# Placing the held and the streamed operand of the large products in different parts of SBUF

## The chip, the cores and the metric

One core of a Trainium2 chip runs the whole program. The metric is device time in microseconds (us), the median of a few executions. A profile of one execution gives the time of every instruction on the five engines: TensorE (PE, with its weight loads as PEld), VectorE (DVE), ScalarE (ACT), GpSimd (POOL) and SyncE (SP, which here issues the DMAs).

A product on TensorE has two operands in SBUF. One is loaded into the array first and stays there; this text calls it the held operand (`lhsT` in the code, the weight load of the profile). The other is then streamed through the array (`rhs`). While one product streams, the held operand of the next one is loaded.

## The reference, cut to what matters

```python
x = attn(q, k, v, p)               # 4 x 576 tokens, 8 heads of 64 -> (2304, 512)
h = x @ w_in;  x = (h * cos(h)) @ w_out               # 512 -> 2048 -> 512, float64 weights
P = exp(x @ w_gate - max); 8 times: rows and columns of P normalised   # 8 experts
out = sum_e P[:, e:e+1] * (relu(x @ w1[e]) @ w2[e])   # 512 -> 1024 -> 512 each
```

Products are made at higher than single-pass precision: each operand is kept as two float32r parts, high and low, and a product is three matmuls (high with high, high with low, low with high).

## The kernel before

The program has three parts. **Attention** (about the first 110 us) is interleaved by a hand-written table, `ORDER`, with the start of the second part. **The first feed-forward layer** runs over 4 slices of its hidden width (`u` below `U1`); each takes the 2304 tokens in 8 chunks of 288 columns (`HC`). `in_g1` (L506 to L508) makes the hidden values, `in_g2` (L565) the output, which is summed in `acc`. **The experts** (`u` from 4 to 19: 16 units, two halves of each of 8 experts) take the tokens in 3 chunks (`j`) of 768. `g1_mult` (L723) forms the first product of an expert as 7 block products per chunk (a Strassen-like scheme, `MULTS`), each of 12 matmuls with 384 columns streamed. `out_tile` (L793 to L795) forms the second product, 6 tiles per chunk of 12 matmuls with 512 columns streamed. In the expert loop of `tile_kernel` a tile of the chunk before stands behind each of the block products 2 to 7 of a chunk (none behind the first), so TensorE's order is: block product, block product, tile, block product, tile, and so on.

The operands of these products:

- in `g1_mult` the held operand is a piece of `w1` (`w_slot`), the streamed one a piece of the transformed tokens (`x_slot`, four of them, refilled by two DMAs each from `xd` in DRAM, `x_load`);
- in `out_tile` the held operand is a piece of the hidden values, out of one of six slots (`slots`: three tiles `slot0` to `slot2` and three pieces of `hreg`), which `relu_split` fills by one ACT and one DVE instruction; the streamed one is `w2` (`whi`, `wlo` of pool `wp`);
- in `in_g2` the held operand is `whi` or `wlo`, the streamed one `hreg`; in `in_g1` both are in `xh` and `xl`.

In the profile the streamed operand is named first: `bank<-whi,hreg` streams `whi` and holds `hreg`. `xh` and `xl` have four planes of 2304 columns. Planes 0 and 1 hold the attention weights of the tokens and later the four `x_slot`s (and, in their last 768 columns, `w_slot`s 9 to 11); planes 2 and 3 hold the mixed weights of the first layer and later `w_slot`s 0 to 8.

Pools are placed from the low end of a partition upward, or from the high end downward (`side="right"`). In the built program of before, the buffers lie at these bytes of each partition:

| buffer | bytes | role in the large products |
|---|---|---|
| `xh`, `xl` | 1,152 to 74,880 | both operands of L506 to L508 and of L723 |
| `hreg` | 77,696 to 100,736 | streamed in L565, held in L793 to L795 |
| `whi`, `wlo` (6 each) | 102,592 to 114,880, 114,880 to 127,168 | held in L565, streamed in L793 to L795 |
| `pp`, `rbuf`, `tail`, `mag`, `val`, later `slot0` to `slot2` | 139,456 to 158,656 | slots: held in L793 to L795 |
| sums, `acc`, first-layer `w1` pieces, raw `w1` (right side) | 161,760 to 229,344 | few products |

Of the kernel before, what the change touches and what calls it, by code (L numbers as in the profile page):

```python
# [8 lines left out]
F32 = mybir.dt.float32  # L9
F32R = mybir.dt.float32r  # L10
# [4 lines left out]
ALU = mybir.AluOpType  # L15
# [3 lines left out]
P = 128  # L19
B, H, S, HD = 4, 8, 576, 64  # L20
NP = 32
NT, DM = 2304, 512
KD = DM // P
# [4 lines left out]
HC = 288  # L28

HT = 384  # L30
NJ = 3
TQ = HT // P
# [72 lines left out]
def tile_kernel(ctx: ExitStack, tc: tile.TileContext, qT, kT, v, pT, w_in, w_out, w_gate, w1, w2, out):  # L105
    nc = tc.nc

    const = ctx.enter_context(tc.tile_pool(name="const", bufs=1))
    small = ctx.enter_context(tc.tile_pool(name="small", bufs=2))
    wp = ctx.enter_context(tc.tile_pool(name="wp", bufs=6))  # L110
    pools = {"w1h": ctx.enter_context(tc.tile_pool(name="w1hp", bufs=6, side="right"))}
# [2 lines left out]

    xh = const.tile([P, KD, NT], F32R, name="xh")
    xl = const.tile([P, KD, NT], F32R, name="xl")
    ident = const.tile([P, P], F32, name="ident")
    ones = const.tile([P, P], F32, name="ones")  # L120
    wg = const.tile([P, KD, E], F32, name="wg")
# [1 line left out]
    lg = const.tile([P, NT // P, E], F32, name="lg")  # L123
    prob = const.tile([P, NT // P, E], F32, name="prob")
    bank = psp.tile([P, 8, 512], F32, name="bank")
    hreg = const.tile([P, 5 * 4 * HC], F32R, name="hreg")
    first = ctx.enter_context(ExitStack())
    cvp = first.enter_context(tc.tile_pool(name="cvp", bufs=1))
    pp = cvp.tile([P, KD, B, 64], F32, name="pp")
# [97 lines left out]
    class Attention:  # L227
# [179 lines left out]
            return x[:, g, S * b:S * b + S]  # L407

        def f_hi(self, i):
            nc.scalar.copy(self.f_dst(xh, i), self.g[i]["a2T"])  # L410

        def f_lo(self, i):
            nc.vector.tensor_tensor(
                out=self.f_dst(xl, i), in0=self.g[i]["a2T"],
                in1=self.f_dst(xh, i).bitcast(F32), op=ALU.subtract,
            )


# [1 line left out]
    def mix_col(b):  # L420
        return S * b + 64 * (b % 2)
# [2 lines left out]


    def pp_hi(j):
        x = (xh, xl)[j // 2][:, 2 + j % 2, :]
        return x.rearrange("p (a s) -> p a s", s=2 * S)[:, :, 512:512 + P]

    def mix_split(j):  # L430
        full = pp[:, j].rearrange("p (a b) n -> p a (b n)", a=2)
        nc.scalar.copy(pp_hi(j), full)
        nc.vector.tensor_tensor(
            out=pools["ppl"][:, j], in0=full, in1=pp_hi(j).bitcast(F32), op=ALU.subtract
        )

    def mix_mm(ps, u, m):
        if u < 2:
            b, g = divmod(m, 2)
# [12 lines left out]
        nc.tensor.matmul(ps, lhsT=pl, rhs=wh, start=False, stop=True)  # L452

    def mix_parts(u, m):
        if u < 2:
            b, g = divmod(m, 2)
            return [(slice(0, P), 2 + g, slice(mix_col(b), mix_col(b) + 512))]
        bp, j = divmod(m, KD)
        parts = []
        for h in range(2):  # L460
            o = mix_col(2 * bp + (h ^ (j % 2)))
            parts.append((slice(64 * h, 64 * h + 64), 2 + j // 2, slice(o, o + 512)))
        return parts

    def mix_hi(ps, u, m):
        for rows, plane, cols in mix_parts(u, m):
            nc.scalar.copy(xh[rows, plane, cols], ps[rows, :])

    def mix_lo(ps, u, m):
        for rows, plane, cols in mix_parts(u, m):  # L470
            nc.vector.tensor_tensor(
                out=xl[rows, plane, cols], in0=ps[rows, :],
                in1=xh[rows, plane, cols].bitcast(F32), op=ALU.subtract,
            )

    def acc_cols(t0, n):

        i, o = divmod(t0, NA)
        return acc[i].rearrange("p (k n) -> p k n", n=NA)[:, :, o:o + n]

    h_sb = {}
# [4 lines left out]
    def ps_g1(s):  # L486
        return pair(g1_pair.get(s, s % 2))
# [5 lines left out]
    def unit_step(s):  # L493
        return s // 16, (s % 16) // 2, s % 2

    def in_g1(s):
        u, c, p = unit_step(s)
        ps = ps_g1(s)
        t0 = HC * c
        for fi in range(2):  # L500
            o = mix_col(c // 2) + P * (2 * p + fi)
            for g in range(2):
                mh, ml = xh[:, 2 + g, o:o + P], xl[:, 2 + g, o:o + P]
                ah, al = xh[:, g, t0:t0 + HC], xl[:, g, t0:t0 + HC]
                dst = ps[:, fi, 0:HC]
                nc.tensor.matmul(dst, lhsT=mh, rhs=ah, start=(g == 0), stop=False)  # L506
                nc.tensor.matmul(dst, lhsT=mh, rhs=al, start=False, stop=False)
                nc.tensor.matmul(dst, lhsT=ml, rhs=ah, start=False, stop=(g == 1))  # L508

    def in_hi(s):  # L510
        u, c, p = unit_step(s)
# [69 lines left out]

    def x_slot(n):
        cols = slice(HT * n, HT * n + HT)
        return xh[:, 0:2, cols], xl[:, 0:2, cols]

    def w_slot(q):
        r, o = (2, 256 * q) if q < 9 else (0, 4 * HT + 256 * (q - 9))
        return xh[:, r:r + 2, o:o + 256], xl[:, r:r + 2, o:o + 256]


    def way_slot(z):
        cols = slice(1024 + HT * z, 1024 + HT * z + HT)
        return xh[:, 2:4, cols], xl[:, 2:4, cols]

    xd = ctx.enter_context(tc.tile_pool(name="xdp", bufs=1, space=bass.MemoryType.DRAM)).tile(
        [7 * NJ, P, 2, 2 * HT], F32, name="xd"
# [5 lines left out]
    def halves(t):  # L602
        return t.rearrange("p (a n) -> p a n", a=2)
# [99 lines left out]
        put(2, a12)  # L703

    def next_h():
        slot = slots.pop(0)
        return slot, halves(slot[:, 0:2 * HT]), halves(slot[:, 2 * HT:4 * HT])

    def two_banks(b):
        return bank[:, 2 * b:2 * b + 2, 0:HT]  # L710
# [16 lines left out]
        x_load()  # L727

    def relu_split(src, th, q, hb):
        slot, hi, lo = next_h()  # L730
        nc.scalar.activation(hi, src, AF.Relu)  # L731
        nc.vector.scalar_tensor_tensor(
            out=lo, in0=src, scalar=0.0, in1=hi.bitcast(F32), op0=ALU.max, op1=ALU.subtract
        )
        hb[q, th] = (hi, lo, slot)

    def g1_steps(u, j):

# [34 lines left out]
    def out_g2(u, j, i):  # L773
        parts = 2 if u == NU - 1 and j == NJ - 1 and i == 2 * TQ - 1 else 1
        for part in range(parts):
            out_tile(u, j, i, part, KD // parts)
        if i % TQ == TQ - 1:
            slots.extend(h_sb[u, j][q, i // TQ][2] for q in range(2))

    def out_tile(u, j, i, part, width):  # L780

        t = 2 * TQ * j + i
        e, half = divmod(u - U1, 2)
        planes = slice(part * width, part * width + width)
        ps = bank[:, 4 + counts["bank"] % 3, 0:P * width]
        counts["bank"] += 1
        th, o = divmod(i, TQ)
        for f in range(4):
            wh, wl = (w[:, P * planes.start:P * planes.stop] for w in w_sb[u, 2, f])
            p, q = divmod(f, 2)  # L790
            hi, lo, _ = h_sb[u, j][q, th]
            a, bq = hi[:, p, P * o:P * o + P], lo[:, p, P * o:P * o + P]
            nc.tensor.matmul(ps, lhsT=a, rhs=wh, start=(f == 0), stop=False)  # L793
            nc.tensor.matmul(ps, lhsT=a, rhs=wl, start=False, stop=False)  # L794
            nc.tensor.matmul(ps, lhsT=bq, rhs=wh, start=False, stop=(f == 3))  # L795
        ps = ps.rearrange("p (k n) -> p k n", n=P)
        dst = acc_cols(P * t, P)[:, planes, :]
        if e == 0:
            if half == 0:
                nc.scalar.copy(dst, ps)  # L800
            else:
                nc.vector.tensor_tensor(out=dst, in0=ps, in1=dst, op=ALU.add)
            return
# [70 lines left out]
    side = []  # L874
# [9 lines left out]
    with tc.manual_schedule():  # L884
# [14 lines left out]
        def in_front(s):  # L899
            in_g1(s)  # L900
            in_turns(s)
            if s > 0:
                in_hi(s - 1)
                in_lo(s - 1)
            if s >= 4:
                in_acc(s - 4)
            in_rest(s)
            if s in convert:
                convert[s]()
# [147 lines left out]
        in_acc(n1 - 4)  # L1057
        first.close()
        op = ctx.enter_context(tc.tile_pool(name="op", bufs=1))
        slots = [op.tile([P, 4 * HT], F32R, name=f"slot{i}") for i in range(3)]  # L1060
        slots += [hreg[:, 4 * HT * i:4 * HT * i + 4 * HT] for i in range(3)]
        l_sb = op.tile([P, HT], F32, name="l_sb")


# [91 lines left out]
```

## Time and profile before

| | |
|---|---|
| median of 3 runs | 1926.49 us (1925.85 to 1928.16) |
| the profiled execution | 1925.82 us, of which its span from first to last instruction is 1924.0 us |
| TensorE busy | 1890.1 us of the span (98%), 11113 matmuls |
| DVE, ACT, POOL busy | 952.2, 595.6 and 505.1 us |
| chain that ended last | TensorE 77% of the span: L723 36%, L793 to L795 41% |
| mean granted TensorE clock | 0.995 of full |

The profile's page gives busy times and groups of instructions; the busy time of TensorE counts matmuls that overlap, and the end of each matmul is modelled, so the mean duration of a matmul is no measure of its pace. The pace is read from the timeline, as the distance between the starts of successive matmuls.

### The profile page before, as it was taken

How to read it: one execution, taken by the hardware profiler on the slowest of the kernel's cores; microseconds unless marked ns; L12 is line 12 of the kernel's file. 1: busy time of each engine (PE TensorE's matmuls, PEld its weight loads, DVE VectorE, ACT ScalarE, POOL GpSimd, SP SyncE). 2: the span in 40 equal slices, each digit the busy share in tenths (PEclk: the TensorE clock that was granted, in tenths of full speed). 3: DMA queues.
4: the chain of work that ended last, by engine and by line, in shares of the span. 5: the costliest groups of instructions: out<-in, count | busy, mean ns of one | idle time of the engine just before them, and what ended most of it. 6: DMA issues, size and time to landing. Idle time of an engine off the chain costs nothing.

```text
span 1924.0 us, 27227 instructions
## 1 busy us (share of the span) xinstructions
PE 1890.1 (98%) x11113; PEld 1711.4 (89%) x11113; DVE 952.2 (49%) x1239; ACT 595.6 (31%) x911; POOL 505.1 (26%) x382
## 2 busy tenths in 40 slices
PE   6999999988999999999999999999999999999999
PEld 4799999977998999989999999999899989999998
DVE  6867776564554563444434343434344443434343
ACT  5877777632321121212122121212121212121210
POOL 3445454520322222221212131303030303030300
PEclk9999999999999999999999999999999999999999
DMA  8511111189665656565666666666666666656564
GB/s 297 159 45 56 45 55 45 58 270 306 198 224 169 228 173 225 172 226 182 214 196 208 200 191 203 201 203 188 204 204 204 196 209 188 215 181 216 185 200 116
DMA packets 229772, 348.89 MB, mean 181 GB/s; under 512 B 14480, under 2 KB 209168, under 8 KB 229648
## 3 DMA queue, kind: packets, MB, share of 16 engines
q1 hardware_dynamic: 229648, 347.15, 56.4%
q8 instruction: 88, 1.44, 0.3%
q14 instruction: 36, 0.29, 0.0%
HBM read 325.86 MB, written 21.23 MB: 180 GB/s over the span
## 4 chain that ended last, share of the span: by engine, by line
PE 77%; DVE 2%; DMA 1%; ACT 1%; POOL 0%; issue 0%; SPq 0%; POOLq 0%; DVEq 0%; ACTq 0%
PE bank L723 36%; PE bank L794 14%; PE bank L793 14%; PE bank L795 13%; DMA xd<-xl 1%; DVE xl L620 1%; DMA xd<-xh 0%; DVE sum L613 0%; DVE rbuf L533 0%; ACT rbuf L538 0%; ACT rbuf L541 0%; DVE rbuf L546 0%; DVE acc L576 0%; PE bank L825 0%; PE bank L565 0%
## 5 line engine op out<-in xcount | busy, mean ns | idle before, releaser
L723 PE MATMUL bank<-xh 128*128 128x384 f32 x1344 | 456.1, 339 | 2.5 <-DVE rbuf L546 2.5
L723 PE MATMUL bank<-xl,xh 128*128 128x384 f32 x1344 | 453.4, 337 | 0.0
L723 PE MATMUL bank<-xh,xl 128*128 128x384 f32 x1344 | 453.0, 337 | 0.0
L747 DVE TENSOR_TENSOR sum<-bank,sum 128x768 f32<-128x768 f32 x240 | 229.8, 957 | 382.8 <-PE bank L723 382.7
L681 POOL TENSOR_TENSOR xl<-wraw,xh 128x512 fp32r<-128x512 f32 x112 | 158.1, 1412 | 701.8 <-ACT xh L680 646.2
L806 DVE SCALAR_TENSOR_TENSOR acc<-bank,prob,acc 128x512 f32<-128x512 f32 (+1 forms) x253 | 189.0, 747 | 189.9 <-PE bank L795 188.8
L723 PEld LDWEIGHTS bank<-xh 128*128 128x128 f32 x1344 | 253.2, 188 | 19.1 <-issue 3.7
L723 PEld LDWEIGHTS bank<-xl,xh 128*128 128x128 f32 x1344 | 253.7, 189 | 10.0
L723 PEld LDWEIGHTS bank<-xh,xl 128*128 128x128 f32 x1344 | 253.4, 189 | 0.0
L794 PE MATMUL bank<-wlo,hreg 128*128 128x512 f32 x580 | 228.1, 393 | 0.0
L795 PE MATMUL bank<-whi,hreg 128*128 128x512 f32 x580 | 226.1, 390 | 0.0
L793 PE MATMUL bank<-whi,hreg 128*128 128x512 f32 x580 | 225.8, 389 | 0.0
L793 PE MATMUL bank<-whi,slot 128*128 128x512 f32 x576 | 224.8, 390 | 0.0
L794 PE MATMUL bank<-wlo,slot 128*128 128x512 f32 x576 | 224.7, 390 | 0.0
L795 PE MATMUL bank<-whi,slot 128*128 128x512 f32 x576 | 224.1, 389 | 0.0
L223 POOL TENSOR_TENSOR wlo<-raw,whi 128x512 fp32r<-128x512 f32 x64 | 86.8, 1367 | 440.0 <-ACT whi L222 440.0
L565 PE MATMUL bank<-hreg,whi 128*128 128x288 f32 x1024 | 187.0, 294 | 0.2 <-DVE rbuf L546 0.2
L731 ACT ACTIVATE hreg<-sum 128x768 fp32r<-128x768 f32 x72 | 61.0, 847 | 374.3 <-DVE sum L747 374.3
L731 ACT ACTIVATE slot<-sum 128x768 fp32r<-128x768 f32 x72 | 60.9, 846 | 369.6 <-DVE sum L747 369.6
L565 PEld LDWEIGHTS bank<-hreg,whi 128*128 128x128 f32 x1024 | 153.1, 188 | 2.0 <-DVE rbuf L546 1.1
L795 PEld LDWEIGHTS bank<-whi,hreg 128*128 128x128 f32 x580 | 108.9, 188 | 23.7
L795 PEld LDWEIGHTS bank<-whi,slot 128*128 128x128 f32 x576 | 108.1, 188 | 23.2
(143 smaller groups left out, 2482.0 us busy)
## 6 DMA issues: line engine op xcount, KB each, us to landing
xh<-xd SPq DMA_DIRECT2D x332, 384.0 KB, 3.4
xl<-xd SPq DMA_DIRECT2D x332, 384.0 KB, 4.0
raw<-w SPq DMA_DIRECT2D x32, 512.0 KB, 6.0
wraw<-w SPq DMA_DIRECT2D x64, 256.0 KB, 5.1
raw<-w_in SPq DMA_DIRECT2D x16, 512.0 KB, 3.7
raw<-w_out SPq DMA_DIRECT2D x16, 512.0 KB, 3.7
xd<-xh SPq DMA_DIRECT2D x21, 384.0 KB, 5.1
xd<-xl SPq DMA_DIRECT2D x21, 384.0 KB, 5.5
```

Of the source, the lines that this page charges most:

```text
L223: nc.gpsimd.tensor_tensor(out=lo, in0=raw, in1=hi.bitcast(F32), op=ALU.subtract)
L565: nc.tensor.matmul(ps[:, di, 0:HC], lhsT=lhsT, rhs=rhs, start=(n in (0, 6)), stop=(n in (17, 23)),)
L620: nc.vector.tensor_tensor(out=lo, in0=src[m], in1=hi.bitcast(F32), op=ALU.subtract)
L681: nc.gpsimd.tensor_tensor(out=lo, in0=src, in1=hi.bitcast(F32), op=ALU.subtract)
L723: nc.tensor.matmul(dst, lhsT=w, rhs=t[:, k, :], start=start and k == 0 and w is a and t is th, stop=k == 1 and w is bq, skip_group_check=True,
L731: nc.scalar.activation(hi, src, AF.Relu)
L747: nc.vector.tensor_tensor(out=out, in0=ps, in1=other, op=ALU.add)
L793: nc.tensor.matmul(ps, lhsT=a, rhs=wh, start=(f == 0), stop=False)
L794: nc.tensor.matmul(ps, lhsT=a, rhs=wl, start=False, stop=False)
L795: nc.tensor.matmul(ps, lhsT=bq, rhs=wh, start=False, stop=(f == 3))
L806: nc.vector.scalar_tensor_tensor(out=dst, in0=ps, scalar=prob[:, t, e:e + 1], in1=dst, op0=ALU.mult, op1=ALU.add)
```

## The change

`xh` and `xl` are taken apart. Planes 0 and 1 become `ah` and `al`, planes 2 and 3 become `mh` and `ml`. `ah`, `al` and `hreg` go into a new pool `upper` at the high end of the partition; `mh` and `ml` stay at the low end. `hreg` grows from 5760 to 6144 columns, so that it has four slots for the experts in place of three. The other two slots for hidden values are now columns 1536 to 2304 of `ah` and `al`, where `w_slot`s 9 to 11 were; those move into a new tile `more`, low in the partition, on the bytes that `pp`, `rbuf` and part of `tail` leave free when the first layer ends. `slot0` to `slot2` are gone.

```diff
     const = ctx.enter_context(tc.tile_pool(name="const", bufs=1))
+    upper = ctx.enter_context(tc.tile_pool(name="upper", bufs=1, side="right"))
...
-    xh = const.tile([P, KD, NT], F32R, name="xh")
-    xl = const.tile([P, KD, NT], F32R, name="xl")
+    ah = upper.tile([P, 2, NT], F32R, name="ah")
+    al = upper.tile([P, 2, NT], F32R, name="al")
+    hreg = upper.tile([P, 16 * HT], F32R, name="hreg")
+    mh = const.tile([P, 2, NT], F32R, name="mh")
+    ml = const.tile([P, 2, NT], F32R, name="ml")
...
-    hreg = const.tile([P, 5 * 4 * HC], F32R, name="hreg")
...
     def x_slot(n):
         cols = slice(HT * n, HT * n + HT)
-        return xh[:, 0:2, cols], xl[:, 0:2, cols]
+        return ah[:, :, cols], al[:, :, cols]
 
     def w_slot(q):
-        r, o = (2, 256 * q) if q < 9 else (0, 4 * HT + 256 * (q - 9))
-        return xh[:, r:r + 2, o:o + 256], xl[:, r:r + 2, o:o + 256]
+        if q < 9:
+            cols = slice(256 * q, 256 * q + 256)
+            return mh[:, :, cols], ml[:, :, cols]
+        rest = more[:, q - 9]
+        return halves(rest[:, 0:512]), halves(rest[:, 512:1024])
...
-        slots = [op.tile([P, 4 * HT], F32R, name=f"slot{i}") for i in range(3)]
-        slots += [hreg[:, 4 * HT * i:4 * HT * i + 4 * HT] for i in range(3)]
+        more = op.tile([P, 3, 1024], F32R, name="more")
+        slots = [(ah[:, :, HT * i:HT * i + HT], al[:, :, HT * i:HT * i + HT]) for i in (4, 5)]
+        for i in (3, 0, 1, 2):
+            slot = hreg[:, 4 * HT * i:4 * HT * i + 4 * HT]
+            slots.append((halves(slot[:, 0:2 * HT]), halves(slot[:, 2 * HT:4 * HT])))
```

The rest of the diff renames: what read or wrote planes of `xh` and `xl` now names `ah`, `al`, `mh`, `ml`.

Every engine carries out the same instructions in the same order with the same shapes as before; no matmul, DMA or vector instruction is added, removed or moved. Apart from names, the built programs differ in a handful of waits at the start of the experts: the first write of `more` on ACT waits for GpSimd's last use of `rbuf` (L522 of before), where the first write of `slot0` did; two of DVE's writes into the new fourth piece of `hreg` and its first write of `l_sb` wait for GpSimd as well; GpSimd loses one wait for TensorE.

The bytes of each partition after the change:

| buffer | bytes | role in the large products |
|---|---|---|
| `mh`, `ml` | 1,152 to 38,016 | held in L506 to L508 and in L723 |
| `whi`, `wlo` | 42,688 to 54,976, 54,976 to 67,264 | held in L565, streamed in L793 to L795 |
| `pp`, `rbuf`, `tail`, `mag`, `val`, later `more` | 79,552 to 98,752 | `more`: held in L723 |
| sums, `acc`, first-layer `w1` pieces, raw `w1` | 100,320 to 167,904 | few products |
| `ah`, `al` | 167,904 to 204,768 | streamed in L506 to L508 and in L723; two slots held in L793 to L795 |
| `hreg` | 204,768 to 229,344 | streamed in L565; four slots held in L793 to L795 |

## Rows read from the trace of the kernel before

**Rows 1.** The page: span, busy us per engine (share, instructions), TensorE's granted clock.

```profile
span 1924.0 us, 27227 instructions
PE 1890.1 (98%) x11113; PEld 1711.4 (89%) x11113; DVE 952.2 (49%) x1239; ACT 595.6 (31%) x911; POOL 505.1 (26%) x382
...
PEclk9999999999999999999999999999999999999999
```

**Rows 2.** The page's chain that ended last: shares of the span by engine and line.

```profile
PE 77%; DVE 2%; DMA 1%; ACT 1%; POOL 0%; issue 0%; SPq 0%; POOLq 0%; DVEq 0%; ACTq 0%
PE bank L723 36%; PE bank L794 14%; PE bank L793 14%; PE bank L795 13%; DMA xd<-xl 1%; DVE xl L620 1%; DMA xd<-xh 0%; DVE sum L613 0%; DVE rbuf L533 0%; ACT rbuf L538 0%; ACT rbuf L541 0%; DVE rbuf L546 0%; DVE acc L576 0%; PE bank L825 0%; PE bank L565 0%
```

**Rows 3.** TensorE's waits: who waited for whom, us in total, times, longest.

```profile
PE bank L825 <- DVE lg L816: 7.5, 5, 5.6
PE bank L267 <- DMA k<-kT: 6.6, 3, 4.4
...
PE bank L723 <- DVE rbuf L546: 2.5, 1, 2.5
```

**Rows 4.** The page's costliest groups: out<-in, shapes, count | busy us, mean ns.

```profile
L723 PE MATMUL bank<-xh 128*128 128x384 f32 x1344 | 456.1, 339 | 2.5 <-DVE rbuf L546 2.5
...
L793 PE MATMUL bank<-whi,hreg 128*128 128x512 f32 x580 | 225.8, 389 | 0.0
L793 PE MATMUL bank<-whi,slot 128*128 128x512 f32 x576 | 224.8, 390 | 0.0
...
L565 PE MATMUL bank<-hreg,whi 128*128 128x288 f32 x1024 | 187.0, 294 | 0.2 <-DVE rbuf L546 0.2
L731 ACT ACTIVATE hreg<-sum 128x768 fp32r<-128x768 f32 x72 | 61.0, 847 | 374.3 <-DVE sum L747 374.3
L731 ACT ACTIVATE slot<-sum 128x768 fp32r<-128x768 f32 x72 | 60.9, 846 | 369.6 <-DVE sum L747 369.6
```

**Rows 5.** Timeline of TensorE in the experts (start us, modelled us): beginnings of groups of 12.

```profile
997.11 0.39 PE L793 MATMUL bank<-whi,slot 128*128 128x512 f32 x1
...
999.84 0.34 PE L723 MATMUL bank<-xh 128*128 128x384 f32 x1
...
1001.95 0.33 PE L723 MATMUL bank<-xh 128*128 128x384 f32 x1
...
1004.03 0.39 PE L793 MATMUL bank<-whi,hreg 128*128 128x512 f32 x1
...
1006.78 0.34 PE L723 MATMUL bank<-xh 128*128 128x384 f32 x1
...
1018.61 0.39 PE L793 MATMUL bank<-whi,slot 128*128 128x512 f32 x1
...
1021.33 0.34 PE L723 MATMUL bank<-xh 128*128 128x384 f32 x1
```

**Rows 6.** The same timeline: a tile that begins in `hreg` and alternates with a slot.

```profile
706.67 0.39 PE L793 MATMUL bank<-whi,hreg 128*128 128x512 f32 x1
...
707.37 0.40 PE L793 MATMUL bank<-whi,slot 128*128 128x512 f32 x1
...
708.07 0.39 PE L793 MATMUL bank<-whi,hreg 128*128 128x512 f32 x1
...
708.76 0.39 PE L793 MATMUL bank<-whi,slot 128*128 128x512 f32 x1
...
709.44 0.34 PE L723 MATMUL bank<-xh 128*128 128x384 f32 x1
```

**Rows 7.** The same timeline: 24 matmuls of L565, from their first to the next L723.

```profile
400.90 0.43 PE L565 MATMUL bank<-hreg,whi 128*128 128x288 f32 x2
...
404.06 0.34 PE L723 MATMUL bank<-xh 128*128 128x384 f32 x1
```

**Rows 8.** Timelines of POOL, ACT and DVE where the experts start.

```profile
390.53 1.43 POOL L522 TENSOR_TENSOR hreg<-rbuf,hreg 128x576 fp32r<-128x576 f32 x1 [3.03 <-ACT hreg L516]
...
405.41 0.62 ACT L680 CAST xh<-wraw 128x512 fp32r<-128x512 f32 x1
...
415.86 0.96 DVE L732 SCALAR_TENSOR_TENSOR slot<-sum,slot 128x768 fp32r<-128x768 f32 x1 [1.79 <-ACT slot L731]
```

More of the change, by code (lines that the diff above doesn't have):

```diff
@@ L409, in f_hi @@
         def f_hi(self, i):
-            nc.scalar.copy(self.f_dst(xh, i), self.g[i]["a2T"])
+            nc.scalar.copy(self.f_dst(ah, i), self.g[i]["a2T"])
         def f_lo(self, i):
             nc.vector.tensor_tensor(
-                out=self.f_dst(xl, i), in0=self.g[i]["a2T"],
-                in1=self.f_dst(xh, i).bitcast(F32), op=ALU.subtract,
+                out=self.f_dst(al, i), in0=self.g[i]["a2T"],
+                in1=self.f_dst(ah, i).bitcast(F32), op=ALU.subtract,
             )
@@ L426, in pp_hi @@
     def pp_hi(j):
-        x = (xh, xl)[j // 2][:, 2 + j % 2, :]
+        x = (mh, ml)[j // 2][:, j % 2, :]
         return x.rearrange("p (a s) -> p a s", s=2 * S)[:, :, 512:512 + P]
@@ L456, in mix_parts @@
             b, g = divmod(m, 2)
-            return [(slice(0, P), 2 + g, slice(mix_col(b), mix_col(b) + 512))]
+            return [(slice(0, P), g, slice(mix_col(b), mix_col(b) + 512))]
         bp, j = divmod(m, KD)
@@ L461, in mix_parts @@
             o = mix_col(2 * bp + (h ^ (j % 2)))
-            parts.append((slice(64 * h, 64 * h + 64), 2 + j // 2, slice(o, o + 512)))
+            parts.append((slice(64 * h, 64 * h + 64), j // 2, slice(o, o + 512)))
         return parts
@@ L466, in mix_hi @@
         for rows, plane, cols in mix_parts(u, m):
-            nc.scalar.copy(xh[rows, plane, cols], ps[rows, :])
+            nc.scalar.copy(mh[rows, plane, cols], ps[rows, :])
     def mix_lo(ps, u, m):
@@ L471, in mix_lo @@
             nc.vector.tensor_tensor(
-                out=xl[rows, plane, cols], in0=ps[rows, :],
-                in1=xh[rows, plane, cols].bitcast(F32), op=ALU.subtract,
+                out=ml[rows, plane, cols], in0=ps[rows, :],
+                in1=mh[rows, plane, cols].bitcast(F32), op=ALU.subtract,
             )
@@ L502, in in_g1 @@
             for g in range(2):
-                mh, ml = xh[:, 2 + g, o:o + P], xl[:, 2 + g, o:o + P]
-                ah, al = xh[:, g, t0:t0 + HC], xl[:, g, t0:t0 + HC]
+                wh, wl = mh[:, g, o:o + P], ml[:, g, o:o + P]
+                th, tl = ah[:, g, t0:t0 + HC], al[:, g, t0:t0 + HC]
                 dst = ps[:, fi, 0:HC]
-                nc.tensor.matmul(dst, lhsT=mh, rhs=ah, start=(g == 0), stop=False)
-                nc.tensor.matmul(dst, lhsT=mh, rhs=al, start=False, stop=False)
-                nc.tensor.matmul(dst, lhsT=ml, rhs=ah, start=False, stop=(g == 1))
+                nc.tensor.matmul(dst, lhsT=wh, rhs=th, start=(g == 0), stop=False)
+                nc.tensor.matmul(dst, lhsT=wh, rhs=tl, start=False, stop=False)
+                nc.tensor.matmul(dst, lhsT=wl, rhs=th, start=False, stop=(g == 1))
     def in_hi(s):
@@ L583, in x_slot @@
         cols = slice(HT * n, HT * n + HT)
-        return xh[:, 0:2, cols], xl[:, 0:2, cols]
+        return ah[:, :, cols], al[:, :, cols]
     def w_slot(q):
-        r, o = (2, 256 * q) if q < 9 else (0, 4 * HT + 256 * (q - 9))
-        return xh[:, r:r + 2, o:o + 256], xl[:, r:r + 2, o:o + 256]
+        if q < 9:
[3 more added lines that the diff above has]
+        return halves(rest[:, 0:512]), halves(rest[:, 512:1024])
     def way_slot(z):
         cols = slice(1024 + HT * z, 1024 + HT * z + HT)
-        return xh[:, 2:4, cols], xl[:, 2:4, cols]
+        return mh[:, :, cols], ml[:, :, cols]
     xd = ctx.enter_context(tc.tile_pool(name="xdp", bufs=1, space=bass.MemoryType.DRAM)).tile(
@@ L705, in next_h @@
     def next_h():
-        slot = slots.pop(0)
-        return slot, halves(slot[:, 0:2 * HT]), halves(slot[:, 2 * HT:4 * HT])
+        return slots.pop(0)
     def two_banks(b):
@@ L729, in relu_split @@
     def relu_split(src, th, q, hb):
-        slot, hi, lo = next_h()
+        hi, lo = next_h()
         nc.scalar.activation(hi, src, AF.Relu)
@@ L734, in relu_split @@
         )
-        hb[q, th] = (hi, lo, slot)
+        hb[q, th] = (hi, lo)
     def g1_steps(u, j):
@@ L777, in out_g2 @@
         if i % TQ == TQ - 1:
-            slots.extend(h_sb[u, j][q, i // TQ][2] for q in range(2))
+            slots.extend(h_sb[u, j][q, i // TQ] for q in range(2))
     def out_tile(u, j, i, part, width):
@@ L790, in out_tile @@
             p, q = divmod(f, 2)
-            hi, lo, _ = h_sb[u, j][q, th]
+            hi, lo = h_sb[u, j][q, th]
             a, bq = hi[:, p, P * o:P * o + P], lo[:, p, P * o:P * o + P]
```

## The prediction, made before the changed kernel ran

> **What bounds the kernel now.** The page comes first: TensorE is busy for 98% of the span and its granted clock stands at full in every slice [rows 1], which is the upper of its two levels, 2.4 GHz. The chain that ended last lies on TensorE for 77% of the span, 36% in L723 and 41% in L793 to L795 [rows 2]. TensorE's waits come next: the three largest are 7.5, 6.6 and 2.5 us, all at the start of the program or of the experts [rows 3]. So in the experts, some 1500 us, nothing but the pace of the matmuls sets the time, and a change that only moves buffers can act in one way alone: it changes that pace.
>
> The grouped view doesn't show the pace. It gives 389 and 390 ns for a 512-column matmul that holds `hreg` or a slot [rows 4], but these ends are modelled and the matmuls overlap. The starts in the timeline do show it. A block product (12 matmuls of 384 columns) that follows another block product takes 1004.03 - 1001.95 = 2.08 us, or 173.3 ns a matmul. One that follows a tile takes 1001.95 - 999.84 = 2.11 [rows 5]. Tiles (12 matmuls of 512 columns) come in four kinds, by the places of their held operands: all in slots 1021.33 - 1018.61 = 2.72 us, which is 226.7 ns a matmul; slot first, then `hreg`, 999.84 - 997.11 = 2.73; all in `hreg` 1006.78 - 1004.03 = 2.75 [rows 5]; `hreg` first, then slot, 709.44 - 706.67 = 2.77 [rows 6]. The instructions are the same; the addresses differ, and so does what ran just before. What the chip does with these addresses is what the change plays on.
>
> **The change, part by part.** No instruction is added, removed or moved on any engine, so the sum is made of paces alone. Call "together" a pair in which the streamed operand and the held operand that is loaded meanwhile both lie below byte 127,168 or both above 139,456, and "apart" the rest. In before, all-slot tiles are apart and all-`hreg` tiles together; L723 is together throughout. After, every pair inside a block product or a tile is apart (`mh`, `ml`, `more`, `whi`, `wlo` end at 93,000 or below, `ah`, `al`, `hreg` begin at 167,904).
>
> Tiles. There are 48 chunks (16 units, 3 each) of 6, so 288 tiles; the six slots rotate so that the four kinds are a quarter each. Over the 2.72 of the all-slot kind they cost 0, 0.01, 0.03 and 0.05 us, on average 0.0225: 288 x 0.0225 = 6.5 us to be had [rows 5, 6].
>
> Block products. 48 x 7 = 336, of which one in seven follows another directly and the first chunk has no tiles: some 282 follow a tile. The excess is 2.11 - 2.08, in steps of 0.01; I take 0.025, and 282 x 0.025 = 7.1 us [rows 5]. So 13.6 us lie over the smooth pace in all.
>
> The boundaries. Not all of it goes. The two products have their roles crossed: L723 holds low and streams high, the tiles hold high and stream low. At each change from one to the other the last streamed operand and the first new held one lie together: `ah` streams while a slot loads, `whi` streams while `mh` loads. In before, the tiles that begin with such a pair are the two kinds that begin in `hreg`. The all-`hreg` tile prices it from below: its later groups of three go at 0.69 against 0.68 us, so of its 0.03 excess about 0.02 is the steady part and about 0.01 is the beginning. The `hreg`-first mixed tile prices it from above: of its 0.05, two slow groups of three explain 0.01 to 0.02, and up to 0.035 stays with the beginning; its first six matmuls take 708.07 - 706.67 = 1.40 against 1.36 at the smooth pace [rows 6]. The other end is zero: a block product that follows a block product is together and smooth. I take 0.01 for each of the 288 + 282 boundaries, from the all-`hreg` tile, whose later pairs are of one kind as they will be after: 5.7 us stay.
>
> First layer. 2304 matmuls of 288 columns. Their pace is (404.06 - 400.90) / 24 = 131.7 ns, all together [rows 7]. From 173.3 ns at 384 columns to 226.7 at 512 the smooth pace rises by 0.417 ns a column; at 288 it would be 133.3. So the first layer is no slower than smooth already. Apart, it might come to that line (+1.6 ns x 2304 = +3.7 us) or gain as much; I take 0 and keep both ends.
>
> Other engines. ACT writes a slot in 846 ns and a piece of `hreg` in 847 [rows 4], so their place costs ACT nothing. The new waits are for GpSimd's last uses of `rbuf` and `hreg`, over by 392 us of the span (390.53 + 1.43); the first write of `w_slot` 9 comes at 405.41 and the third write of a slot at 415.86 [rows 8], more than 13 us later. They cost nothing; if GpSimd were later than that, the excess would come on the path once.
>
> The sum: 13.6 - 5.7 = 7.9 us off the profiled execution's 1925.82 (span 1924.0 and 1.8 around it): 1917.9. The median of the runs shown lies 0.7 above that execution, so the forecast is 1918 us. With its own unknowns, boundaries at 0 and the first layer at either end, the likeliest case spans 1912 to 1923.
>
> **The rivals.** *Boundaries free and the pace better still.* If the apart pairs are wholly smooth and the boundaries cost nothing, all 13.6 us go: 1913. With the first layer's 3.7 as well, 1909; a few us less if the smooth pace itself falls. For it: the all-slot tile, smooth from its first matmul although it follows another product. Against it: that tile's first pair is apart, which no boundary will be after.
>
> *The halves do nothing.* Block product after block product is together and as smooth as anything in the trace [rows 5], and a mixed tile is rough in its slot part too, where the pairs are apart: 708.07 - 707.37 = 0.70 against 0.68 [rows 6]. So roughness may come from what ran before, and it would only be dealt out anew. Price: nothing gone 1926; boundaries at 0.035 for tiles and 0.025 for block products 13.6 - 10.1 - 7.1 = -3.6, so 1930. Span 1923 to 1930. The Trainium skill (SBUF — State Buffer, Who interferes with whom) gives TensorE two independent read ports, one for the streamed operand and one for weight loads, and says that it never waits on anyone. By that rule the place of the operands could not matter and the time would stay at 1926; the trace agrees where block products follow each other and does not where an `hreg` tile and a slot tile differ by 0.03 us with the same instructions.
>
> *Slower: the offset, not the half.* The smooth pairs have something else in common: the same offset within 512 bytes. `whi` (102,592) and `slot0` (139,456) are both at 192, L723's operands (from 1,152 on) all at 128, while `hreg` (77,696) is at 384 beside `whi`'s 192. After the change no large product keeps equal offsets: 480 for `ah` and `hreg` (167,904, 204,768), 128 for `mh`, 192 for `whi`. If that is what makes a tile rough, every tile becomes an all-`hreg` one (288 x (0.03 - 0.0225) = +2.2 us), and L723 pays 0.03 / 12 = 2.5 ns on each of 4032 matmuls (+10.1 us) on top of what it pays: 1939. It decides from where a block product after a block product takes 2.10 or more. Against it: 288-column matmuls, with offsets of every kind, are at 131.7, under their line; that also makes a smaller loss likely, so I span 1931 to 1939.
>
> **How the numbers follow.** Forecast 1918 with 0.42, boundaries free 0.16, nothing 0.25, offsets 0.17. About 0.2% (3.9 us) is what a measurement of this kernel can tell from no change: faster is below 1922.6, slower above 1930.3. The first two cases are faster, 0.58; the third is the same, 0.25; the fourth slower, 0.17. For 8 in 10 the range takes the first three and leaves out the fourth and the lowest end: 1907 to 1930.
>
> **What would show it.** Right: in the experts a tile takes 2.72 to 2.73 whichever slots it holds, and a block product after a tile 2.09; the four kinds of tile merge into one. Boundaries free: 2.72 and 2.08 everywhere. Nothing: tiles that begin on a rough boundary, 2.75 or more for all, block products at 2.11 still. Offsets: block products over 2.10 also where they follow each other. The first layer is read from 24 matmuls of L565: 3.16 now, 3.20 on the smooth line. The granted clock must stay where it is; if a wait on GpSimd shows up at the first write of `more`, the new waits were not free. The forecast is wrong if the pace depends on something that the old placement holds constant, which this trace cannot show.

## The result, and the profile after

The changed kernel takes 1946.68 us, median of 4 runs (1943.77 to 1947.09); the kernel before took 1926.17 beside it. The ratio is 1.0104 (95% interval 1.0087 to 1.0122): 1% slower, where 0.4% faster was forecast, and above the top of the range. The profiled execution took 1947.09 us, its span 1945.3, 21.3 more than [rows 1].

The page of the changed kernel, with the span, the engines' busy us, TensorE's granted clock, and the head of the chain that ended last:

```profile
span 1945.3 us, 27228 instructions
...
PE 1914.1 (98%) x11113; PEld 1719.7 (88%) x11113; DVE 952.9 (49%) x1239; ACT 596.2 (31%) x911; POOL 504.9 (26%) x382
...
PEclk9999999999999999999999999999999999999999
...
PE 77%; DVE 2%; DMA 1%; ACT 1%; POOL 0%; issue 0%; SPq 0%; DVEq 0%; ACTq 0%; POOLq 0%
```

Against [rows 1, 2] only TensorE's busy time has grown, by 24.0 us; DVE, ACT and POOL are within 0.7 us, the clock is full in every slice (mean 0.996, was 0.995), and the chain has the same shares by engine. The one instruction more in the count is none that computes: VectorE has three more semaphore instructions, ScalarE and GpSimd one fewer each. TensorE's waits show no new entry that matters (columns as in [rows 3]):

```profile
PE bank L833 <- DVE lg L824: 8.7, 5, 6.8
...
PE bank L731 <- DVE rbuf L552: 1.1, 1, 1.1
```

So the same matmuls at the same clock are spaced more widely. TensorE's timeline in the experts, the first matmul of each group of 12 (columns as in [rows 5]; L731 is the old L723, L801 the old L793):

```profile
702.92 0.39 PE L801 MATMUL bank<-whi,ah 128*128 128x512 f32 x1
...
705.71 0.34 PE L731 MATMUL bank<-ah,mh 128*128 128x384 f32 x1
...
1001.77 0.39 PE L801 MATMUL bank<-whi,hreg 128*128 128x512 f32 x1
...
1004.56 0.34 PE L731 MATMUL bank<-ah,mh 128*128 128x384 f32 x1
...
1006.67 0.39 PE L801 MATMUL bank<-whi,hreg 128*128 128x512 f32 x1
...
1009.46 0.34 PE L731 MATMUL bank<-ah,more 128*128 128x384 f32 x1
...
1011.58 0.34 PE L731 MATMUL bank<-ah,mh 128*128 128x384 f32 x1
...
1013.71 0.39 PE L801 MATMUL bank<-whi,hreg 128*128 128x512 f32 x1
```

Every tile takes 2.79 us, whether it begins in `ah` (705.71 - 702.92) or in `hreg` (1004.56 - 1001.77). The four kinds have become one, but above the worst of the old ones (2.77), not at the best. A block product that follows another takes 1013.71 - 1011.58 = 2.13 here and 2.12 on average, where [rows 5] had 2.08; one that follows a tile takes 2.11 to 2.12.

The distances of all matmul starts add up as follows. Tiles: 13.3 us more (288 tiles by 2.79 against a mean of 2.7425 would give 13.7). Block products: 3.2 us more, the net of some 5 in pace (their means per 12 rose from 2.081 to 2.119 behind another one, 46 undisturbed ones, and from 2.106 to 2.118 behind a tile, 268) and some 2 less around one wait at the start of the experts, which the layout does not explain (last section). First layer: 1.7 us over 2304 matmuls. All the rest of the program: 2.9 us, of which 1.7 lie in the first 175 us, attention above all, and 1.2 in the wait for `lg` above. That makes 21.1 of the 21.3.

### The profile page after: what moved, and what is told of

It is laid out like the page before. It is cut to its first block, busy times and chain, and to the rows that moved or that the text cites. A ratio compares the mean times of both kernels' runs of the same rounds, so it can differ in the third digit from the quotient of the medians.

```text
span 1945.3 us, 27228 instructions
## 1 busy us (share of the span) xinstructions
PE 1914.1 (98%) x11113; PEld 1719.7 (88%) x11113; DVE 952.9 (49%) x1239; ACT 596.2 (31%) x911; POOL 504.9 (26%) x382
## 4 chain that ended last, share of the span: by engine, by line
PE 77%; DVE 2%; DMA 1%; ACT 1%; POOL 0%; issue 0%; SPq 0%; DVEq 0%; ACTq 0%; POOLq 0%
PE bank L731 36%; PE bank L803 14%; PE bank L802 14%; PE bank L801 14%; DMA xd<-ml 1%; DVE ml L629 0%; DMA xd<-mh 0%; DVE acc L582 0%; PE bank L833 0%; DVE sum L622 0%; DMA al<-xd 0%; DVE rbuf L539 0%; ACT rbuf L544 0%; ACT rbuf L547 0%; DVE rbuf L552 0%
## 5 line engine op out<-in xcount | busy, mean ns | idle before, releaser
L731 PE MATMUL bank<-ah,mh 128*128 128x384 f32 x1020 | 347.2, 340 | 1.1 <-DVE rbuf L552 1.1
L731 PE MATMUL bank<-al,mh 128*128 128x384 f32 x1020 | 346.2, 339 | 0.0
L731 PE MATMUL bank<-ah,ml 128*128 128x384 f32 x1020 | 345.5, 339 | 0.0
L803 PE MATMUL bank<-whi,hreg 128*128 128x512 f32 (+1 forms) x796 | 314.4, 395 | 0.0
L802 PE MATMUL bank<-wlo,hreg 128*128 128x512 f32 (+1 forms) x796 | 313.2, 394 | 0.0
L801 PE MATMUL bank<-whi,hreg 128*128 128x512 f32 (+1 forms) x796 | 312.3, 392 | 0.0
L739 ACT ACTIVATE hreg<-sum 128x768 fp32r<-128x768 f32 x96 | 81.2, 846 | 466.0 <-DVE sum L755 466.0
L731 PEld LDWEIGHTS bank<-ah,mh 128*128 128x128 f32 x1020 | 192.3, 189 | 14.7 <-issue 3.7
L731 PEld LDWEIGHTS bank<-al,mh 128*128 128x128 f32 x1020 | 192.5, 189 | 9.3
L731 PEld LDWEIGHTS bank<-ah,ml 128*128 128x128 f32 x1020 | 192.0, 188 | 0.0
L803 PEld LDWEIGHTS bank<-whi,hreg 128*128 128x128 f32 x796 | 149.6, 188 | 34.4
L731 PE MATMUL bank<-ah,more 128*128 128x384 f32 x648 | 179.4, 339 | 0.0
L801 PEld LDWEIGHTS bank<-whi,hreg 128*128 128x128 f32 x796 | 149.5, 188 | 25.7
```

Of the source, the lines that this page charges most:

```text
L731: nc.tensor.matmul(dst, lhsT=w, rhs=t[:, k, :], start=start and k == 0 and w is a and t is th, stop=k == 1 and w is bq, skip_group_check=True,
```

## The experiments

The rival on offsets was the only one that had put the time above 1930.3, so the experiments set it against the halves. Buffers are moved by unused tiles ("pads") ahead of them; no instruction differs. Offsets are given modulo 256 bytes from here on; why 256 is shown below. Line numbers of the timeline rows are those of the kernel in question: L723 and L793 of before are L725 and L795 in its padded versions.

**All offsets equal, in both placements.** In the first kernel the halves are as in the changed kernel, in the second as in before; in both, every operand of every large product lies at 128.

```diff
     hreg = upper.tile([P, 16 * HT], F32R, name="hreg")
+    upper.tile([P, 88], F32, name="pad1")
...
     prob = const.tile([P, NT // P, E], F32, name="prob")
+    const.tile([P, 112], F32, name="pad2")
```

> The changed kernel with two unused pieces of SBUF put in, 352 bytes at the top of the upper pool and 448 bytes ahead of the small pools, so that every large operand (ah, al, hreg, mh, ml, whi, wlo, more) begins at 128 within 512 bytes; the halves stay as the change has them. Offset theory (a pair is smooth when streamed and held operand have the same offset within 512 bytes, wherever they lie): block products 2.08 us, tiles 2.72 us, about 20 + 14 us below the changed kernel's 1946: 1912. Theory that the upper half, or lying apart, is itself slow: the paces stay at 2.12 and 2.79, 1946.

```diff
+    const.tile([P, 64], F32, name="pad1")
     hreg = const.tile([P, 5 * 4 * HC], F32R, name="hreg")
+    const.tile([P, 48], F32, name="pad2")
```

> The kernel before with hreg, whi, wlo and the slots all moved to offset 128 within 512, which xh and xl have already; the halves as before (hreg with whi together, slots apart, block products together). Offset theory: tiles 2.72 and block products 2.08, also where one follows the other, since the pair at the boundary is equal too: 1912, and the same as the changed kernel with equal offsets. Theory of the halves: block products and hreg tiles stay rough, 1926.

Measured: 1931.46 us (1928.84 to 1936.03; ratio 1.0025, 1.0014 to 1.0037) and 1933.3 us (1928.82 to 1934.27; ratio 1.0031, 1.0018 to 1.0044). TensorE's timeline, of the changed placement first, then of the old one:

```profile
1001.46 0.33 PE L733 MATMUL bank<-ah,more 128*128 128x384 f32 x1
...
1003.57 0.33 PE L733 MATMUL bank<-ah,mh 128*128 128x384 f32 x1
...
1005.65 0.39 PE L803 MATMUL bank<-whi,hreg 128*128 128x512 f32 x1
...
1008.41 0.33 PE L733 MATMUL bank<-ah,mh 128*128 128x384 f32 x1
```

```profile
1002.63 0.39 PE L795 MATMUL bank<-whi,slot 128*128 128x512 f32 x1
...
1005.40 0.33 PE L725 MATMUL bank<-xh 128*128 128x384 f32 x1
...
1007.50 0.33 PE L725 MATMUL bank<-xh 128*128 128x384 f32 x1
...
1009.58 0.39 PE L795 MATMUL bank<-whi,hreg 128*128 128x512 f32 x1
...
1012.34 0.33 PE L725 MATMUL bank<-xh 128*128 128x384 f32 x1
```

In the changed placement a block product behind a tile takes 2.11, one behind a block product 2.08, a tile 2.76; in the old one 2.10, 2.08 and 2.76 to 2.77. Over all of them the means per 12 matmuls differ by 1 ns at most. Where the offsets agree, it makes no difference whether the two operands lie in one half or in two: the halves theory falls. 15 us of the 20 between the medians come back by moving buffers some hundred bytes.

But both miss the 1912 that was expected. With all pairs equal, tiles ought to have been at 2.72, and they are at 2.76. Within a tile the starts are 229, 233, 236, 224, 231, 236, 228, 232 and 231 ns apart, then 227: the first nine are rough, the last three smooth. So there may be a second cost, of the change from one product to the next. The end of the program separates it: there five tiles follow another tile, with no block product between. TensorE's timeline of the old placement with equal offsets, two of these:

```profile
1920.67 0.39 PE L795 MATMUL bank<-whi,hreg 128*128 128x512 f32 x1
...
1923.39 0.39 PE L795 MATMUL bank<-whi,hreg 128*128 128x512 f32 x1
```

They take 2.72, and so do all five in both kernels: in the same kernel, with the same offsets, the 0.04 us are paid behind a block product and not behind a tile. The next layouts show that this cost is not the same everywhere.

**Equal offsets within each product, one step between them.** `hreg` alone is moved in before, so that it agrees with `whi` and the slots at 192, while block products stay at 128.

```diff
+    const.tile([P, 80], F32, name="pad1")
     hreg = const.tile([P, 5 * 4 * HC], F32R, name="hreg")
+    const.tile([P, 48], F32, name="pad2")
```

> The kernel before with hreg moved up by 320 bytes, so that it has the offset of whi and of the slots (192 within 512); what stands above moves by 512. hreg and whi still lie together in the lower half. Offset theory: all four kinds of tile at 2.72 us (2.72 to 2.77 before), block products as they were (2.08 behind another, 2.11 behind a tile): 288 x 0.024 = 7 us less, 1919. Theory of the halves: tiles with hreg stay rough, 2.73 to 2.77, 1926.

Measured: 1921.42 us (1916.58 to 1923.95), ratio 0.9971 (0.9960 to 0.9983). The timeline of TensorE:

```profile
994.68 0.34 PE L725 MATMUL bank<-xh 128*128 128x384 f32 x1
...
996.78 0.33 PE L725 MATMUL bank<-xh 128*128 128x384 f32 x1
...
998.87 0.39 PE L795 MATMUL bank<-whi,hreg 128*128 128x512 f32 x1
...
1001.59 0.34 PE L725 MATMUL bank<-xh 128*128 128x384 f32 x1
...
1013.35 0.39 PE L795 MATMUL bank<-whi,slot 128*128 128x512 f32 x1
...
1016.07 0.34 PE L725 MATMUL bank<-xh 128*128 128x384 f32 x1
```

All tiles take 2.72, those in `hreg` (1001.59 - 998.87) too, although these operands still lie in one half; 6.5 us had been worked out for that, and by the sum of all starts 7.0 are gone from the tiles. Block products behind a tile stay at 2.10.

**The changed kernel's offsets, in before's places.** `hreg` and the slots go to 224 beside `whi` at 192, as `ah` and `hreg` stand to `whi` after the change. The slots are still in the other half, `hreg` still in the same.

```diff
+    const.tile([P, 24], F32, name="pad1")
     hreg = const.tile([P, 5 * 4 * HC], F32R, name="hreg")
+    const.tile([P, 104], F32, name="pad2")
...
+        op.tile([P, 72], F32, name="pad3")
         slots = [op.tile([P, 4 * HT], F32R, name=f"slot{i}") for i in range(3)]
```

> The kernel before with hreg and the three slots moved to offset 480 within 512 and whi and wlo left at 192: the offsets of the changed kernel's tiles, with hreg still together with whi in the lower half and the slots apart from it. Offset theory: every tile at 2.79 us as in the changed kernel, whether it holds hreg or a slot; 288 x (2.79 - 2.744) = 13 us more, 1939. Theory of the halves: slot tiles stay at 2.72 and the time at 1926.

Measured: 1943.83 us (1943.35 to 1944.79), ratio 1.0089 (1.0066 to 1.0112). The timeline of TensorE:

```profile
1006.93 0.40 PE L795 MATMUL bank<-whi,slot 128*128 128x512 f32 x1
...
1009.73 0.33 PE L725 MATMUL bank<-xh 128*128 128x384 f32 x1
...
1011.83 0.34 PE L725 MATMUL bank<-xh 128*128 128x384 f32 x1
...
1013.91 0.40 PE L795 MATMUL bank<-whi,hreg 128*128 128x512 f32 x1
...
1016.71 0.33 PE L725 MATMUL bank<-xh 128*128 128x384 f32 x1
```

Tiles take 2.79 on average (2.79 to 2.80 by these starts), in either half; block products, whose operands were left at 128, keep their 2.08 and 2.10. The changed kernel's tiles are made here by 32 bytes, with no half exchanged. The time is 4.8 us above the 1939 expected: of the 18.9 us by which the span is longer than that of before, the tiles make 14.4, the first layer 1.4 and the small products 2.9.

**Which distances are rough.** Two more versions of before, whose pads (in the same three places) are 64, 448 and 128 bytes, and 352, 160 and 64. By the addresses modulo 512, `whi` stays at 192; in the first version `hreg` is at 448 and the slots at 320, in the second they are at 224 and 256.

> The kernel before with whi and wlo at 192 within 512 as they were, hreg at 448 (256 bytes off) and the slots at 320 (128 bytes off). It asks with what period the offset counts. If it counts within 256 bytes: tiles all in hreg are smooth, 2.72 us, tiles all in slots rough, 2.74 or more. If within 512: both rough. If within 128: both smooth. If it is not the offset at all but the place: hreg tiles 2.75 and slot tiles 2.72 as in before. Block products 2.08 and 2.11 in all cases.

> The kernel before with whi and wlo at 192 within 512, hreg at 224 (held operand 32 bytes above the streamed one) and the slots at 256 (64 above). Offset theory: both rough. The changed kernel holds 32 bytes off (480 against 192, which is 32 within 256) and takes 2.79; so hreg tiles should be at 2.79, slot tiles between 2.74 and 2.79. If only the half or the pool counted: 2.75 and 2.72.

Measured: 1931.48 us (1930.33 to 1932.79; ratio 1.0018, 1.0007 to 1.0028) and 1939.8 us (1938.99 to 1940.62, 2 runs; ratio 1.0062, 1.0042 to 1.0082). The timeline of TensorE in the first:

```profile
1000.34 0.39 PE L795 MATMUL bank<-whi,slot 128*128 128x512 f32 x1
...
1003.13 0.34 PE L725 MATMUL bank<-xh 128*128 128x384 f32 x1
...
1005.21 0.33 PE L725 MATMUL bank<-xh 128*128 128x384 f32 x1
...
1007.30 0.39 PE L795 MATMUL bank<-whi,hreg 128*128 128x512 f32 x1
...
1010.02 0.34 PE L725 MATMUL bank<-xh 128*128 128x384 f32 x1
```

The all-`hreg` tile is smooth, 2.72: 256 bytes apart count as equal. The slots, 128 from `whi`, cost 2.78 to 2.79. In the second kernel tiles in `hreg` take 2.79, as they did at 480 in the kernel ahead, again 256 bytes away; tiles in slots take 2.80. Put together, by how far the held operand lies above the streamed one modulo 256: 0 is smooth; 32 takes 2.79; 64 takes 2.80; 128 takes 2.78; 192 (`hreg` in before) takes 2.75. Each of these four inequalities costs 1 to 3% of a tile, and the size has no simple order. Only multiples of 32 bytes were tried.

**The step between the products.** In five versions every product is equal in itself, and the tiles stand at 64, 192, 0, 96 and 32, while block products are at 128. The second of these is the kernel of 1921.42 above. Three more are before with pads of 384 and 192 bytes (tiles at 0), of 448 and 192 (tiles at 64), of 224 and 192 (at 96); the fifth has 160 and 192 (at 32).

> The kernel before with hreg, whi, wlo and the slots all at 256 within 512, 128 bytes from xh and xl (128): equal offsets inside each product, another step at the boundaries than the 64 of e2 and the 0 of e5. Theory of the boundary step (the step of the offset from one product to the next sets what a boundary costs: +64 is free for a tile, 0 costs 0.04): the smooth pace holds from the middle of a tile on, 0.68 a group of three, and the beginning of tiles and block products costs something else than in e2 and e5, between 0 and 0.04 each: 1913 to 1935. If the step does not matter: tiles 2.76 as in e5, 1933.

> As e8, with hreg, whi, wlo and the slots at 320 within 512: the step from block product to tile is +192, from tile to block product -192, which is +64 within 256. If +64 within 256 is free in both directions: block products behind a tile 2.08 in place of 2.11 (7 us less than e5), tiles 2.72 to 2.76; 1914 to 1926. If the step back costs the same whatever it is: block products 2.11 still.

> The kernel before with hreg, whi, wlo and slots all at 96 (modulo 256), so a step of +224 from block product to tile and of +32 back. If the price of a step changes evenly between the steps measured (+192: 12 ns, +256 or 0: 41 ns; back +64: 2 ns, 0: 26 ns), a tile takes 2.745 and a block product after a tile 2.093: 1923 (1919 to 1927). If a step of +64 is a kind of its own (another row of the memory) and smaller ones count as none: tile 2.76, block product after tile 2.106: 1931.

> The kernel before with hreg, whi, wlo and slots all at 32 (modulo 256), so a step of +160 from block product to tile and of +96 back. If the price of a step changes evenly between those measured (+128: 30 ns, +192: 12 ns; back +64: 2 ns, +128: 30 ns), a tile takes 2.74 and a block product after a tile 2.096: 1923 (1919 to 1927). If the price has its smallest value between the steps tried, under 1917.

With the two kernels at 128 this gives the table below; the last column adds the two extras over 2.72 and 2.08, from the means of all starts.

| tiles at | a tile | a block product behind a tile | both extras, ns | time, us | ratio to before (95%) |
|---|---|---|---|---|---|
| 192 | 2.719 | 2.107 | 26 | 1921.42 | 0.9971 (0.9960 to 0.9983) |
| 128 | 2.760 | 2.106 | 66 | 1933.3 | 1.0031 (1.0018 to 1.0044) |
| 0 | 2.750 | 2.110 | 60 | 1930.56 | 1.0011 (1.0002 to 1.0021) |
| 96 | 2.727 | 2.092 | 19 | 1919.8 | 0.9964 (0.9951 to 0.9977) |
| 64 | 2.732 | 2.082 | 14 | 1917.29 | 0.9948 (0.9931 to 0.9964) |
| 32 | 2.765 | 2.087 | 52 | 1928.14 | 1.0007 (0.9997 to 1.0017) |

The times follow the sum of the extras: from 14 to 66 ns, times some 280, is 15 us, and the times are 16 apart. What sets each price is not settled. It doesn't change evenly with the step: at 96 a tile takes less than at 64 and at 128, at 32 more than at 0 and at 64, so that this last kernel missed its 1923. Nor is it the step alone: in the kernel with `hreg` at 448 and the slots at 320, a block product behind an all-`hreg` tile, which is equal, takes 2.107 and behind the others 2.085 to 2.092.

**The changed kernel with the best offsets.** Its halves stay as they are; block products are put at 128, tiles at 64.

```diff
-    ah = upper.tile([P, 2, NT], F32R, name="ah")
-    al = upper.tile([P, 2, NT], F32R, name="al")
+    ah = upper.tile([P, 2, NT + 64], F32R, name="ah")
+    al = upper.tile([P, 2, NT + 64], F32R, name="al")
+    upper.tile([P, 48], F32, name="pad1")
     hreg = upper.tile([P, 16 * HT], F32R, name="hreg")
+    upper.tile([P, 40], F32, name="pad2")
...
+    const.tile([P, 32], F32, name="pad3")
...
+        op.tile([P, 16], F32, name="pad4")
         more = op.tile([P, 3, 1024], F32R, name="more")
-        slots = [(ah[:, :, HT * i:HT * i + HT], al[:, :, HT * i:HT * i + HT]) for i in (4, 5)]
+        cols = [slice(HT * i + 48, HT * i + HT + 48) for i in (4, 5)]
+        slots = [(ah[:, :, c], al[:, :, c]) for c in cols]
```

> The changed kernel, its halves kept as they are, but with offsets as in the best layout of before so far: all operands of a block product at 128 (modulo 256 bytes), all operands of a tile at 64. Offsets theory: it takes what that layout took, 1917 (1914 to 1921), 0.5% under the kernel before; block product after block product 2.08, block product after tile 2.08, every tile 2.73, whichever slots. Halves theory (apart costs something that equal offsets can't take away): above 1924, with block products or tiles slower than those of that layout by 0.01 us or more per 12 matmuls.

Measured: 1917.01 us (1916.71 to 1917.88), ratio 0.9948 (0.9933 to 0.9963), span 1914.9. The timeline of TensorE:

```profile
994.39 0.39 PE L804 MATMUL bank<-whi,hreg 128*128 128x512 f32 x1
...
997.12 0.33 PE L734 MATMUL bank<-ah,more 128*128 128x384 f32 x1
...
999.20 0.33 PE L734 MATMUL bank<-ah,mh 128*128 128x384 f32 x1
...
1001.28 0.39 PE L804 MATMUL bank<-whi,hreg 128*128 128x512 f32 x1
...
1020.54 0.39 PE L804 MATMUL bank<-whi,ah 128*128 128x512 f32 x1
...
1023.27 0.33 PE L734 MATMUL bank<-ah,mh 128*128 128x384 f32 x1
```

Tiles 2.73 in both places, block products 2.08 everywhere: the paces of the old placement with these offsets, and its time to 0.3 us. All the 30 us between the changed kernel and this one come of moving buffers within their halves.

## Why the prediction was wrong

**What bounds the kernel** was right: TensorE's pace alone, with no wait past the start of the experts and no other engine in it. The clock stayed where it was, but for some 3 us at the start of the experts (last section). One reading was incomplete: behind 7.5 and 6.6 us the full list of waits has 4.2 and 3.9 ahead of the 2.5 that was called the third largest; they too lie at the start of the program and of the experts, so nothing hangs on it.

**The step that failed** is the one that called pairs together and apart. In [rows 5, 6] the all-slot tile differs from the all-`hreg` tile in its half and in its offset at once (192 beside 192 against 128 beside 192), and the forecast gave the difference to the half. Block product behind block product, together and smooth, spoke against that, and the text said so. The two kernels with equal offsets and the one with the changed offsets in the old places decide it: the half does nothing to these paces (1 ns per 12 matmuls at most), and the offsets move a tile between 2.72 and 2.80.

**Tiles.** Forecast -6.5 us before boundaries; measured +13.3. The rival on offsets had the right cause but +2.2, since it gave every unequal pair the price of the one in [rows 5], 2.75. At 32 bytes a tile takes 2.79, at 64 on the other side 2.80: the term was mis-sized by 11 us, because the tiles of before hold a single unequal distance, and the cheapest of the four that were tried.

**Block products.** Forecast -7.1 before boundaries, for 282 behind a tile (by the trace 268; the others stand behind small products); the offset rival said +10.1 on top of what they pay, from 2.5 ns a matmul. Behind another block product the measured rise is 38 ns per 12, 3.2 a matmul, so the decision point of 2.10 was passed (2.12 to 2.13). But behind a tile the new roughness took the place of the old extra rather than adding to it (2.106 to 2.118), and some 5 us came of both.

**Boundaries.** That one exists was right, its cause was not: at [rows 5] it was read as the last operand and the first lying together. Layouts with the same halves have it at 2.082 and at 2.107 for a block product, and at 2.72 to 2.77 for a tile. In the sum it was 0.01 for each side; in the layouts with equal offsets the two sides together cost 0.014 to 0.066.

**First layer.** The line of 3.20 us for 24 matmuls was hit: in the timeline of the changed kernel they begin at 401.65 and the next block product at 404.85, against 3.16 in [rows 7]:

```profile
401.65 0.42 PE L571 MATMUL bank<-hreg,whi 128*128 128x288 f32 x2
...
404.85 0.34 PE L731 MATMUL bank<-ah,more 128*128 128x384 f32 x1
```

Over the whole layer it is half as much, 0.8 ns a matmul (from 132.2 to 133.0) and 1.7 us, between the 0 taken and the end of 3.7. The other layouts lie between, at 132.4 to 132.9 ns, in no order that the runs explain.

**Other engines.** Right: ACT's writes take 846 ns on average (L739, now 96 into `hreg`), as in [rows 4], and no wait of GpSimd's appears on TensorE. But the margin was misread. The write at 405.41 is that of `w_slot` 11; those of 9 and 10 stand ahead of it. In the changed kernel ACT writes `more` first at 394.71:

```profile
394.71 1.14 ACT L689 CAST more<-wraw 128x512 fp32r<-128x512 f32 x2
```

GpSimd's last use of `rbuf` ends there at 394.16, so the margin is 0.55 us and not 13. That the new wait was free was partly luck: ACT was at work on the cast ahead of it and did not idle.

**The rest.** 2.9 us outside the large products were not foreseen. Versions of before with other pads spread as far there (99.4 us in before, 97.4 to 102.2 in its padded versions, 102.3 after), so the halves need not be the cause; what is was not tried. A small slip besides: 1917.9 and the 0.7 by which the median lies higher make 1918.6, not 1918.

**The offset rival's total** came nearest, 1939 against 1946.68, with a chance of 0.17. In part that was luck: its tiles were 11 us too cheap and its block products 5 us or more too dear. Its evidence against itself, the 288-column matmuls at 131.7 with offsets of every kind, was weak: their pace hardly moves in any layout. The Trainium skill (SBUF — State Buffer, Who interferes with whom) gives TensorE two independent read ports and says that it never waits on anyone, from which the prediction concluded that placement could not matter. For the halves the runs agree with that conclusion. For the offsets they don't: 2.72 and 2.80 us for the same 12 matmuls, with only the addresses different.

## What to carry to other kernels

Where matmuls follow one another without a gap and each loads a held operand of its own, read their pace from the starts in the timeline, not from mean durations, and treat the byte offset of the held and the streamed operand as a parameter: give both the same offset modulo 256 bytes, and try a few steps between products that alternate, because a few unused bytes cost nothing and were worth 0.5% here and 1.5% between the best and the worst. Any change that moves buffers changes these offsets as well, so compare layouts at equal offsets before a gain or a loss is given to anything else. When two readings of the same rows differ by one property each, as half and offset did here, a layout that separates them is needed before either is believed.

## What the hardware showed that was not expected

A matmul of 512 columns whose held operand is loaded while its predecessor streams starts every 226.7 ns (2.72 / 12) if both operands have one offset modulo 256 bytes, and on average every 229.6 to 233.6 ns if not (tiles of 2.755 to 2.803); at 384 columns it is 173.3 against 176.5 (2.118 / 12). These unequal tiles stand behind a block product; the few behind another tile give 228.9 ns at 192 bytes (2.747 / 12) and 233.3 at 32 (2.800 / 12). A change of product costs something of its own: with all operands equal, up to nine matmuls behind it are uneven. Why the offset counts, no run shows.

Which of two other engines begins first goes with almost 3 us on TensorE. The wait of [rows 3] for `rbuf` is 1.1 us in the changed kernel and was 2.5. That is not because TensorE came to it later: in the kernel with the changed offsets in before's places it comes as late (first block product at 388.67, changed kernel 388.59, before 385.02) and waits 2.4. What differs is which of two instructions some 10 us earlier began first, one of GpSimd and one of VectorE. Their timelines, of before and then of after:

```profile
378.63 1.47 POOL L522 TENSOR_TENSOR hreg<-rbuf,hreg 128x576 fp32r<-128x576 f32 x1 [2.51 <-ACT hreg L516]
...
378.83 2.08 DVE L613 TENSOR_TENSOR sum<-acc 128x768 f32<-128x768 f32 x1
```

```profile
382.14 0.96 DVE L622 TENSOR_TENSOR sum<-acc 128x768 f32<-128x768 f32 x1
...
382.15 2.24 POOL L528 TENSOR_TENSOR hreg<-rbuf,hreg 128x576 fp32r<-128x576 f32 x1 [2.71 <-ACT hreg L522]
```

The one that begins second takes longer. In all 13 traces of this case it goes together: where GpSimd begins first, by 11 to 197 ns (8 traces), VectorE's instruction takes 2.08 to 2.23 us and TensorE waits 2.43 to 2.54; where VectorE begins first, by 4 to 14 ns (5 traces), it takes 0.96 and TensorE waits 1.12 to 1.17. Both orders occur in both placements. From the start of VectorE's instruction to the end of the `rbuf` write that TensorE waits for there are 10.92 us before and 9.80 after, so its 1.12 us less reach TensorE. Each kernel has one trace and no run sets the order by itself, so how often either comes, and what decides it, is not shown.

The granted clock behind the wait goes with its length. TensorE's timeline there, of before and then of after (the bracket is the idle time and what ended it):

```profile
389.80 0.44 PE L723 MATMUL bank<-xh 128*128 128x384 f32 x1 [2.54 <-DVE rbuf L546]
...
390.65 0.52 PE L723 MATMUL bank<-xh 128*128 128x384 f32 x1
390.97 0.52 PE L723 MATMUL bank<-xl,xh 128*128 128x384 f32 x1
```

```profile
391.99 0.44 PE L731 MATMUL bank<-ah,mh 128*128 128x384 f32 x1 [1.12 <-DVE rbuf L552]
...
392.45 0.34 PE L731 MATMUL bank<-ah,ml 128*128 128x384 f32 x1
392.62 0.34 PE L731 MATMUL bank<-ah,mh 128*128 128x384 f32 x1
```

Before, the matmuls behind the wait start 320 ns apart (390.97 - 390.65), and the granted clock of 389.8 to 393.2 is 0.55, near the lower of the two levels; after, they start 0.17 us apart and the clock of 391.9 to 395.0 is 1.00. In the other traces it is the same: 0.51 to 0.56 behind the long wait, 1.00 behind the short one. The shorter wait is worth 1.4 us, and ten matmuls at 0.18 in place of 0.32 as much again. So some 2.8 us of the difference between two single executions can come of this alone.
